# Expert tiles combined at the next head, two extra turns in the routing, first products of the dense layer reordered

## The chip, the cores and the metric

One Trainium2 chip, one of its cores. The metric is the device time of one execution of the whole kernel in microseconds (us), lower is better. The core's engines run each its own queue of instructions in order: TensorE (PE; PEld is its weight loads), VectorE (DVE), ScalarE (ACT), GpSimd (POOL) and SyncE (SP, which here only issues transfers). They wait for each other by semaphores.

## The reference

Three stages follow one another: attention with pooled queries, a mixture of experts in which each token takes part or is skipped, and a gated dense layer.

```python
q_pool = q.reshape(B, H, S // 2, 2, D).mean(axis=3)          # B 4, H 8, S 1152, D 64
scores = (1 / sqrt(D)) * q_pool @ k.T ; attn = softmax(scores)
x = (attn @ v) as [2304, 512]
do_compute = x @ w_skip > 0                                   # of these tokens:
e_idx = argmax(x @ w_gate) over 8 experts, gate_w = its softmax weight
y = gate_w * (relu(x @ w1[e]) @ w2[e])                        # w1[e] 512 x 1024, w2[e] 1024 x 512
x = x + y for these tokens, x for the others
out = ((x @ m1) * (x @ m2)) @ w3 @ w_out                      # 512 -> 1024 -> 1024 -> 512
```

## The kernel before

All products are made from fp32 values split into a high and a low part, and three partial products each (high by high, high by low, low by high).

**Attention.** 16 pairs of heads (`p`) with 9 row tiles each (`l`) give 144 steps `i`; the loop runs some steps longer to drain. In a step PE transposes the exponentials of step i-2 (`emit_t`, L305, evacuated by ACT and DVE at L324), makes one part of attention times values (`emit_pv`, L341), and the scores of step i (`emit_s`, L271), whose maximum DVE takes at L282 and whose exponential ACT makes at L294. PE's order in a step is transposes, values, scores.

**Side work.** Two generators are advanced in small turns between the instructions of the steps. `conv` rewrites the weights of the dense layer, which come in 64-bit pairs, as plain fp32 (POOL squares at L96, DVE at L111 to L119, transfers at L83 and L86). `route_ops(b)` routes the tokens of batch b and writes their rows to `x_d`; it starts in step 44 + 36 b for the batches 0, 1 and 2. It yields "P" ahead of a piece with PE products and "D" ahead of a piece with DVE work alone. `side("D")` is called once in each step, after the second group of transposes: if the routing stands at "D", it advances the routing; if it stands at "P", or no routing is under way, it advances `conv`. `side("P")` is called at the end of the steps with l in 8, 0, 1, 3, 4, 5, if the routing stands at "P", and advances the routing. Its products go to the one of two accumulators (`VB`) that the values don't use at that l.

**One-hot blocks.** For each of five groups of up to 128 tokens `build(j)` makes a block `ob` on POOL (L441 and L444, twice each) that marks slot and order of each token; PE multiplies its two halves (L465), and DVE adds the result into `slots` (L467). Two block buffers exist, so blocks 0 and 1 are built at once, at the end of the last D turn ahead of them, and block j+2 after the product of block j. Then come the softmax weights (a D turn) and five turns in which the tokens' rows are transposed, scaled (L490), joined with the gate weight (L493) and stored. The fourth batch is routed after the loop with a `hook` and five block buffers; its blocks are built on DVE, and its products are at L456.

**Between the stages.** `wprime` multiplies w3 by w_out, and `wprime_fill` splits their weights on POOL, from the last pair of the attention on.

**Experts.** `tiles(j)` is a nest of 25 branches `If(T > j)`, where T is the number of expert tiles of 128 tokens (11 for these inputs). The branch is at L920 on every engine. `tile_body(j)` gathers the rows of tile j+2 by POOL, splits the expert's weights if it is a new one, multiplies (`hmm`, `htr`, `ymm`; PE at L560), and at its end combines: DVE adds gate times product from bank B[5] to the row (L743), and POOL scatters the rows to `x_d` (L744). Behind the last tile, the other branch (`Else`) calls `split_m1`: ACT and DVE split the first weights of the dense layer into `W1`, four pieces of two column blocks each (`split_cols`, L912 on ACT, L913 on DVE).

**Dense layer.** The splits of its second weights into `V2` follow (same two lines). `group(g)` takes 384 tokens: for each of eight column blocks c it makes the product with `W1` in one bank and that with `V2` in the next (L952, 12 matmuls each), multiplies both (ACT L955, DVE L956), and splits the result; then it makes the output products (L560) and scatters the rows. The rows of the next group are gathered at the start of a group (`ld_x`, L615). Group 0 holds tokens without an expert.

Of the kernel before, what the change touches and what calls it, by code (L numbers as in the profile page):

```python
# [44 lines left out]
def body(ctx, tc, q, k, v, w9, w1, w2, m1, m2, w3t, wo, cst, mcst, ids, out, dbg=None):  # L45
# [89 lines left out]
    if True:  # L135
# [217 lines left out]
        def route_ops(b, hook=None, obs=None):  # L353
# [93 lines left out]
            parts = ((0, 0, NSL), (1, NSL, NCNT))  # L447
            for j in range(len(obs)):
                build(j)
            if len(obs) == NTT:  # L450
                yield "P"
                tp = tbank()
                for u, c0, n in parts:
                    for j in range(NTT):
                        t = ob[j]
                        PE.matmul(tp[:, c0:c0 + n], lhsT=t[:, 128 * u:128 * u + 128], rhs=t[:, 256 + c0:256 + c0 + n],  # L456
                                  start=(j == 0), stop=(j == NTT - 1))
                DVE.tensor_tensor(slots, tp[:, 0:NSL + NCNT], slots, op=ALU.add)
            else:
                for j in range(NTT):  # L460
                    yield "P"
                    tp = tbank()
                    t = ob.pop(j)
                    for u, c0, n in parts:
                        PE.matmul(tp[:, c0:c0 + n], lhsT=t[:, 128 * u:128 * u + 128], rhs=t[:, 256 + c0:256 + c0 + n],  # L465
                                  start=True, stop=True)
                    DVE.tensor_tensor(slots, tp[:, 0:NSL + NCNT], slots, op=ALU.add)  # L467
                    if j + len(obs) < NTT:
                        build(j + len(obs))
# [30 lines left out]
        def side(kinds):  # L500
            k = rts.get("k")
            if k and k in kinds:
                rts["k"] = next(rts["g"], None)
            elif k != "D":
                next(conv, None)

        def emit_meta(scratch):
# [184 lines left out]
            DVE.tensor_tensor(XTt[1], b0, f(XTt[0]), op=ALU.subtract)  # L692

        def tile_body(j, x2_first):
            xg = XR[j % 4]
            more = j + 1 < NTILE
            if j + 2 < NTILE:
                gather(j + 2)
            if j + 3 < NTILE:
                ld_idx(j + 3)  # L700
            if j:
                nw = nc.values_load(meta[0:1, j, 0:1], min_val=0, max_val=1)
                with tc.If(nw > 0):
                    split(W2, R2, 8)
                    ld_next(R2, w2, j)

            def hmm(hh, a0, a1):
                for a in range(a0, a1):
                    mm3(B[1 + hh], [XTt[0][:, a], XTt[1][:, a]],
                        [W1[x][:, a, 512 * hh:512 * hh + 512] for x in range(2)], a == 0, a == 3)  # L710
                if a1 == 4:
                    ACT.activation(HS[:, 512 * hh:512 * hh + 512], B[1 + hh], AF.Relu)

            def htr(hh):
                for u in range(4):
                    c = 4 * hh + u
                    PE.transpose(B[3 + hh][:, 128 * u:128 * u + 128], HS[:, 128 * c:128 * c + 128], ident)
                b3 = B[3 + hh].rearrange("p (a c) -> p a c", a=4)
                ACT.copy(HT[0][:, 4 * hh:4 * hh + 4], b3)
                DVE.tensor_tensor(HT[1][:, 4 * hh:4 * hh + 4], b3, f(HT[0][:, 4 * hh:4 * hh + 4]), op=ALU.subtract)  # L720

            def ymm(a0, a1):
                for a in range(a0, a1):
                    mm3(B[5], [HT[0][:, a], HT[1][:, a]], [W2[0][:, a], W2[1][:, a]], a == 0, a == 7)

            hmm(0, 0, 4)
            hmm(1, 0, 2)
            htr(0)
            hmm(1, 2, 4)
            if more:  # L730
                xpose(j + 1)
            if j == 0:
                x2_first()
            ymm(0, 2)
            htr(1)
            if more:
                nw = nc.values_load(meta[0:1, j + 1, 0:1], min_val=0, max_val=1)
                with tc.If(nw > 0):
                    split(W1, R1, 4)
                    ld_next(R1, w1, j + 1, "m1")  # L740
            ymm(2, 4)
            ymm(4, 8)
            DVE.scalar_tensor_tensor(xg[:, 0:D], B[5], xg[:, D:D + 1], xg[:, 0:D], op0=ALU.mult, op1=ALU.add)  # L743
            scs.append(POOL.indirect_dma_start(  # L744
                out=x_d[:, :], out_offset=bass.IndirectOffsetOnAxis(ap=IDX[j % 5][:, :], axis=0),
                in_=xg[:, :], in_offset=None, bounds_check=N - 1, oob_is_err=False).ins)

        with tc.manual_schedule():
# [23 lines left out]
            for i in range(NSTEP + 7):  # L772
# [25 lines left out]
                if tr:  # L798
                    for g in range(3):
                        emit_t(it, g, i, evac)  # L800
                        emit_c(it, g, EV[g], evac)
                        if g == 1 and i > 5:
                            side("D")
                if 1 <= i <= NSTEP:
                    emit_e(i - 1)
                for u in pvs:
# [105 lines left out]
                ACT.copy(W[0][:, :, cols], r[:, :, cols])  # L912
                DVE.tensor_tensor(W[1][:, :, cols], r[:, :, cols], f(W[0][:, :, cols]), op=ALU.subtract)  # L913

            def split_m1():
                for c in range(0, 8, 2):
                    split_cols(W1, R1, c, c + 2)

            def tiles(j):
                with tc.If(T > j) as cmp:  # L920
                    tile_body(j, x2_first)
                    if j + 1 < NTILE:
                        tiles(j + 1)
                    else:
                        split_m1()
                with cmp.Else():
                    if j == 0:
                        x2_first()
                    split_m1()
            tiles(0)  # L930

            V2 = [W2[x].rearrange("p a f -> p (a f)").rearrange("p (a f) -> p a f", a=4) for x in range(2)]
# [11 lines left out]
            def group(g, x2, nx):  # L944
                if nx is not None:
                    ld_x(nx, XR)
                for c in range(8):
                    pa, pb = B[(2 * c) % 4], B[(2 * c) % 4 + 1]
                    for o, W in ((pa, W1), (pb, V2)):
                        seq = [(0, y, a) for a in range(4) for y in range(2)] + [(1, 0, a) for a in range(4)]  # L950
                        for n, (x, y, a) in enumerate(seq):
                            PE.matmul(o[:, 0:GT], lhsT=W[x][:, a, 128 * c:128 * c + 128], rhs=x2[y][:, a],  # L952
                                      start=(n == 0), stop=(n == len(seq) - 1))
                    av, cv = AV[c % 2], CW_[c % 2]
                    ACT.copy(av, pa[:, 0:GT])  # L955
                    DVE.tensor_tensor(cv, pb[:, 0:GT], av, op=ALU.mult)  # L956
                    ACT.copy(CV[0][:, c], cv)  # L957
                    DVE.tensor_tensor(CV[1][:, c], cv, f(CV[0][:, c]), op=ALU.subtract)
                    if g == 0 and nx is not None:
                        ACT.copy(WP[0][:, c], WPr[:, c])  # L960
                        DVE.tensor_tensor(WP[1][:, c], WPr[:, c], f(WP[0][:, c]), op=ALU.subtract)
                    if nx is not None and c in (3, 5, 7):
                        x2t(X2[nx % 2], (c - 3) // 2, XR[(c - 3) // 2])
# [82 lines left out]
```

## Time and profile before

| | |
|---|---|
| median of 3 runs | 1090.47 us (1088.94 to 1090.56) |
| profiled execution | 1092.66 us |
| its span, first to last instruction | 1090.8 us |
| busy: PE, DVE, ACT, POOL | 1038.4, 598.0, 482.4, 387.0 us |
| waits of PE for one-hot blocks (L465) | 5.9 us in 3 |
| wait of PE at the first product of the dense layer (L952) | 4.7 us in 1 |
| granted clock of PE, mean over the span | 0.984 |

Times within the trace count from the span's start. The attention stage runs to about 550 us, the experts' tiles from about 615 to 767 us, the dense layer from there to the end. A busy PE is not PE at its peak, since matmuls are pipelined and their ends are modelled; so the length of a piece of work is best read from the distance between starts of the same instruction in neighbouring steps.

### The profile page before, as it was taken

To read this page: it belongs to the slowest core of one execution; us is meant where nothing else is said; L and a number is where in the kernel's file an instruction comes from. 1 tells how busy PE (TensorE), PEld (TensorE's weight loads), DVE (VectorE), ACT (ScalarE), POOL (GpSimd) and SP (SyncE) were. 2 spreads that over 40 slices of the span, in tenths; PEclk is the share of its full clock that TensorE was granted. 3 is DMA by queue.
4 is the path that set the end of the run, shared out by engine and by line. 5 is a ranking of instruction groups with operands and counts; after the bars stand their busy time and mean duration, and the time that the engine had idled before them with its cause. 6 is when DMAs were issued, how large, how long until landed. Compare 5 with 4: busy or idle time off the path is not lost. (4 is left out here: it accounts for less than half of the span.)

```text
span 1090.8 us, 16927 instructions
## 1 busy us (share of the span) xinstructions
PE 1038.4 (95%) x6101; PEld 839.9 (77%) x6101; DVE 598.0 (55%) x934; ACT 482.4 (44%) x902; POOL 387.0 (35%) x426
## 2 busy tenths in 40 slices
PE   6999999999999999999999999998799999999996
PEld 5677776677766777667667778786799998989895
DVE  5888887688986888755637422437531221212120
ACT  4666666565665666555532322334432221212121
POOL 4754433672536724351620523439201010101101
PEclk9999999999999999989998999999899999999999
DMA  9887778377973678714702761507101010101000
GB/s 256 259 239 192 216 218 232 101 182 212 268 224 98 185 214 256 183 40 101 238 20 74 247 225 40 190 25 243 34 11 50 10 49 20 39 20 39 29 2 30
DMA packets 68237, 144.83 MB, mean 133 GB/s; under 512 B 12960, under 2 KB 22560, under 8 KB 68130
## 3 DMA queue, kind: packets, MB, share of 16 engines
q1 hardware_dynamic: 63330, 129.28, 41.1%
q0 software_dynamic: 4800, 14.24, 4.0%
q8 instruction: 53, 0.87, 0.3%
q14 instruction: 54, 0.44, 0.1%
HBM read 86.21 MB, written 22.87 MB: 100 GB/s over the span
## 5 line engine op out<-in xcount | busy, mean ns | idle before, releaser
L282 DVE TENSOR_REDUCE sm<-s 128x1 f32<-128x1152 f32 x144 | 195.2, 1356 | 108.4 <-PE s L271 88.3
L324 ACT COPY pt<-s 128x384 f32<-128x384 f32 x288 | 138.0, 479 | 184.4 <-PE s L305 184.1
L271 PE MATMUL s<-k,q 128*128 128x384 f32 x864 | 204.3, 364 | 15.5 <-DVE k L197 7.8
L271 PEld LDWEIGHTS s<-k,q 128*128 128x128 f32 x864 | 147.2, 193 | 83.8 <-issue 41.7
L294 ACT ACTIVATE p<-s,sm 128x1152 f32<-128x1152 f32 x144 | 176.3, 1225 | 10.0 <-DVE sm L282 9.7
L341 PE MATMUL vb<-pt,vr 128*64 128x256 f32 (+1 forms) x1152 | 173.9, 422 | 4.5 <-DVE xr L490 2.1
L305 PE MATMUL s<-cs,p 128*128 128x128 f32 x1296 | 172.0, 279 | 2.9 <-ACT p L294 2.9
L305 PEld LDWEIGHTS s<-cs,p 128*128 128x128 f32 x1296 | 151.5, 144 | 12.1 <-ACT p L294 6.2
L956 DVE TENSOR_TENSOR ar<-b,ar 128x384 f32<-128x384 f32 x48 | 26.8, 558 | 191.9 <-PE b L952 191.9
L341 PEld LDWEIGHTS vb<-pt,vr 128*64 128x64 f32 x1152 | 70.7, 137 | 59.4 <-issue 23.7
L971 POOL DMA_INDIRECT out_dram<-ar,slots x18 | 18.1, 1003 | 272.1 <-ACT ar L970 267.4
L324 DVE COPY pt<-s 128x384 f32<-128x384 f32 x144 | 78.9, 548 | 5.1 <-PE s L305 5.0
L225 POOL TENSOR_TENSOR kl<-kr,kh 128x384 fp32r<-128x384 f32 x45 | 47.6, 1058 | 73.0 <-DMA k<-kl 70.2
L957 ACT CAST CVh<-ar 128x384 fp32r<-128x384 f32 x48 | 24.6, 513 | 108.8 <-DVE ar L956 108.8
L96 POOL TENSOR_TENSOR cm<-ch 128x512 f32<-128x512 f32 x40 | 43.0, 1079 | 66.6 <-DVE ca L119 46.1
L560 PE MATMUL b<-W1h,CVh 128*128 128x512 f32 x176 | 60.5, 403 | 1.2 <-ACT CVh L691 0.7
L560 PE MATMUL b<-W2h,CVh 128*128 128x512 f32 x176 | 60.7, 405 | 0.3
L560 PE MATMUL b<-WPh,CVh 128*128 128x512 f32 x144 | 57.3, 398 | 0.0
L560 PE MATMUL b<-WPh,CVl 128*128 128x512 f32 x144 | 56.9, 395 | 0.0
L560 PE MATMUL b<-WPl,CVh 128*128 128x512 f32 x144 | 56.8, 395 | 0.0
L970 ACT COPY ar<-b 128x512 f32<-128x512 f32 x18 | 10.6, 586 | 86.2 <-PE b L560 86.2
L224 POOL TENSOR_SCALAR kh<-kr 128x384 fp32r<-128x384 f32 x45 | 27.2, 604 | 57.2 <-PE s L271 53.6
(210 smaller groups left out, 1816.7 us busy)
## 6 DMA issues: line engine op xcount, KB each, us to landing
R<-in_w_dram SPq DMA_DIRECT2D x16, 1024.0 KB, 7.1
vr<-in_v_dram SPq DMA_DIRECT2D x16, 576.0 KB
kr<-in_k_dram SPq DMA_DIRECT2D x15, 576.0 KB, 6.2
qr<-in_q_dram SPq DMA_DIRECT2D x15, 576.0 KB, 6.6
k<-kh SPq DMA_DIRECT2D x30, 288.0 KB, 5.6
k<-kl SPq DMA_DIRECT2D x30, 288.0 KB, 6.4
q<-qnl SPq DMA_DIRECT2D x60, 144.0 KB, 3.4
ch<-in_w3t_dram SPq DMA_DIRECT2D x16, 512.0 KB, 5.6
```

The costliest lines, as they stand in the source:

```text
L96: POOL.tensor_tensor(m, hf, hf, op=ALU.mult)
L224: POOL.tensor_scalar(KH[i][:, cc], rawk[p][:, cc], 1.0, 0.0, op0=ALU.mult, op1=ALU.add)
L225: POOL.tensor_tensor(KL[:, cc], rawk[p][:, cc], f(KH[i][:, cc]), op=ALU.subtract)
L271: m = PE.matmul(sp[:, c, 0:384], lhsT=lt, rhs=kk[:, 384 * c:384 * c + 384], start=(n == 0), stop=(n == len(seq) - 1))
L282: DVE.tensor_reduce(sm, sp[:, :, 0:384], axis=AX.XY, op=ALU.max, negate=True)
L294: ACT.activation(pt, sp[:, :, 0:384], AF.Exp, bias=sm, scale=1.0, accum_out=SM[b][:, hp, c:c + 1])
L305: m = PE.transpose(tp[:, u * 128:u * 128 + 128], src[:, kt * 128:kt * 128 + 128], ident)
L324: m = (DVE.tensor_copy(o, i_) if eng is DVE else ACT.copy(o, i_)).ins
L341: PE.matmul(acc[64 * h:64 * h + 64, 0:n], lhsT=vr[:, h, kt, :], rhs=pt[:, kt, h, :], start=(kt == 0), stop=(kt == KT - 1))
L560: PE.matmul(o, lhsT=lh[a], rhs=rh[b_], start=(first and n == 0), stop=(last and n == len(order) - 1))
L956: DVE.tensor_tensor(cv, pb[:, 0:GT], av, op=ALU.mult)
L957: ACT.copy(CV[0][:, c], cv)
```

## The change

In the first three batches `route_ops` yields twice more, as "C", between the building of the first two blocks and the first product. `side("DC")` advances the routing at "D" and at "C"; `conv` is advanced in each step's call unless the routing stood at "D" (so in a C turn both are), and not at all by `side("P")`. The end of `tile_body` becomes a function `combine(j)`. It is called at the head of `tile_body(j + 1)`, or, behind the last tile, in `split_m1`, after two pieces of one column block each; the other three pieces follow it. In the group 0 that is followed by another group, PE makes the `W1` products of the blocks 0 and 1 ahead of their `V2` products.

```diff
@@ route_ops, side
             for j in range(len(obs)):
                 build(j)
+            if not hook:
+                yield "C"
+                yield "C"
             if len(obs) == NTT:
@@
             if k and k in kinds:
                 rts["k"] = next(rts["g"], None)
-            elif k != "D":
+            if kinds != "P" and k != "D":
                 next(conv, None)
@@ tile_body
         def tile_body(j, x2_first):
-            xg = XR[j % 4]
+            if j:
+                combine(j - 1)
             more = j + 1 < NTILE
@@
             ymm(2, 4)
             ymm(4, 8)
+
+        def combine(j):
+            xg = XR[j % 4]
             DVE.scalar_tensor_tensor(xg[:, 0:D], B[5], xg[:, D:D + 1], xg[:, 0:D], op0=ALU.mult, op1=ALU.add)
             scs.append(POOL.indirect_dma_start(
@@ the loop over the steps
                         if g == 1 and i > 5:
-                            side("D")
+                            side("DC")
@@ split_m1, tiles
-            def split_m1():
-                for c in range(0, 8, 2):
+            def split_m1(j):
+                split_cols(W1, R1, 0, 1)
+                split_cols(W1, R1, 1, 2)
+                if j >= 0:
+                    combine(j)
+                for c in range(2, 8, 2):
                     split_cols(W1, R1, c, c + 2)
@@
                     else:
-                        split_m1()
+                        split_m1(j)
                 with cmp.Else():
                     if j == 0:
                         x2_first()
-                    split_m1()
+                    split_m1(j - 1)
@@ group
-                for c in range(8):
-                    pa, pb = B[(2 * c) % 4], B[(2 * c) % 4 + 1]
-                    for o, W in ((pa, W1), (pb, V2)):
+                def prods(c, which):
+                    for o, W in ((B[(2 * c) % 4 + u], (W1, V2)[u]) for u in which):
                         seq = [(0, y, a) for a in range(4) for y in range(2)] + [(1, 0, a) for a in range(4)]
...
+                for c in range(8):
+                    pa, pb = B[(2 * c) % 4], B[(2 * c) % 4 + 1]
+                    if g == 0 and nx is not None and c < 2:
+                        if c == 0:
+                            prods(0, (0,))
+                            prods(1, (0,))
+                        prods(c, (1,))
+                    else:
+                        prods(c, (0, 1))
```

## Rows read from the trace of the kernel before

**Rows 1.** The page, busy us (share of the span) and instructions of each engine.
```profile
PE 1038.4 (95%) x6101; PEld 839.9 (77%) x6101; DVE 598.0 (55%) x934; ACT 482.4 (44%) x902; POOL 387.0 (35%) x426
```

**Rows 2.** Waits of PE over the span: us in total, times, longest.
```profile
PE vb L465 <- POOL ob L444: 5.9, 3, 2.0
PE b L952 <- DVE W1l L913: 4.7, 1, 4.7
...
PE vb L456 <- DVE R L444: 1.8, 4, 0.5
```

**Rows 3.** Timeline of PE, first batch: start, us, instruction, idle before and releaser.
```profile
207.96 1.34 PE L271 MATMUL s<-k,q 128*128 128x384 f32 x6
211.29 0.75 PE L465 MATMUL vb<-ob 128*128 128x146 f32 x2 [1.99 <-POOL ob L444]
...
215.60 1.34 PE L271 MATMUL s<-k,q 128*128 128x384 f32 x6
...
218.86 1.34 PE L271 MATMUL s<-k,q 128*128 128x384 f32 x6
...
222.32 0.62 PE L271 MATMUL s<-k,q 128*128 128x384 f32 x2
```

**Rows 4.** The same timeline in the second and in the third batch.
```profile
344.54 1.34 PE L271 MATMUL s<-k,q 128*128 128x384 f32 x6
...
352.15 1.32 PE L271 MATMUL s<-k,q 128*128 128x384 f32 x6
...
481.65 1.34 PE L271 MATMUL s<-k,q 128*128 128x384 f32 x6
...
489.63 2.24 PE L271 MATMUL s<-k,q 128*128 128x384 f32 x6
...
493.80 1.31 PE L271 MATMUL s<-k,q 128*128 128x384 f32 x6
...
497.24 0.62 PE L271 MATMUL s<-k,q 128*128 128x384 f32 x2
```

**Rows 5.** Timeline of POOL, first batch: the building of blocks 0 and 1.
```profile
209.17 1.21 POOL L441 TENSOR_SCALAR ob<-iota,hf 128x128 fp32r<-128x128 f32 x2 [7.51 <-DVE hf L434]
...
210.37 1.29 POOL L444 TENSOR_SCALAR ob<-iota,hf,idf 128x146 fp32r<-128x146 f32 x2
```

**Rows 6.** Stretches: length, busy PE, PEld, DVE, ACT, POOL; granted clock, DMA, GB/s.
```profile
211.30:215.20 3.90, 3.81 (x17) 2.92 (x19) 1.50 (x3) 1.56 (x3) 3.90 (x7) 0.56 0.00 0
...
485.00:491.70 6.70, 6.70 (x25) 5.02 (x26) 1.48 (x3) 2.17 (x4) 5.67 (x9) 0.50 0.38 94
...
580.40:587.30 6.90, 6.44 (x19) 5.18 (x20) 5.15 (x22) 0.00 (x0) 0.00 (x0) 0.51 0.01 2
...
771.80:775.00 3.20, 3.19 (x10) 3.20 (x11) 3.20 (x4) 3.14 (x5) 1.37 (x1) 0.50 0.03 8
```

**Rows 7.** Instructions on tile xr, 230 to 545 us: count, ns least/median/most.
```profile
L493 DVE COPY xr<-ga x15: 151/160/1406, 244.0 to 540.3; 128x4 f32<-128x4 f32 x12, 64x4 f32<-64x4 f32 x3
```

**Rows 8.** Timeline of all engines behind the last tile.
```profile
764.97 3.89 ACT L912 CAST W1h<-R 128x1024 fp32r<-128x1024 f32 x4 [3.32 <-issue]
...
767.15 0.75 DVE L743 SCALAR_TENSOR_TENSOR xr<-b,xr 128x512 f32<-128x512 f32 x1 [4.77 <-PE b L560]
...
770.45 4.63 DVE L913 TENSOR_TENSOR W1l<-R,W1h 128x1024 fp32r<-128x1024 f32 x4 [2.55 <-issue]
...
771.82 0.66 PE L952 MATMUL b<-X2h,W1h 128*128 128x384 f32 x1 [4.71 <-DVE W1l L913]
```

**Rows 9.** Branches of PE's queue at L920: whole span, then 766 to 773 us.
```profile
L920 PEldq COMPARE_BRANCH  x13: 65/70/3672, 614.7 to 770.4; - x13
...
L920 PEldq COMPARE_BRANCH  x2: 179/1926/3672, 766.4 to 770.4; - x2
```

**Rows 10.** Timeline around one tile's end: its sum, and the next product into B[5].
```profile
647.34 0.75 DVE L743 SCALAR_TENSOR_TENSOR xr<-b,xr 128x512 f32<-128x512 f32 x1 [2.77 <-PE b L560]
...
653.54 0.49 PE L560 MATMUL b<-W2h,CVh 128*128 128x512 f32 x1
```

## The prediction, made before the changed kernel was run

> **What bounds the kernel now.** I read the page first: TensorE is busy for 95% of the span [rows 1], so only what leaves TensorE idle, or slows it, is worth anything. Then the waits of TensorE over the whole span: two rows of that list belong to lines that the change touches [rows 2]. One is L465, the products of the one-hot blocks, which waited for the POOL builds three times, 5.9 us in all; the other is L952, the first product of the dense layer, which waited once for 4.7 us. Third, the timeline of TensorE around the three waits, to see what they cost beyond the idle time itself [rows 3, 4]; fourth, the table of stretches for the granted clock behind them [rows 6]; last, the timeline and the branches at the change from the experts to the dense layer [rows 8, 9]. [...] And the 4.7 us at the dense layer are for the most part a jump of TensorE's own queue, which the change doesn't shorten.
>
> **Part 1, the two turns.** In each of the first three batches the last D turn ends with POOL building two one-hot blocks, and the first product follows at the end of the same step (step 55 of 144 in the first batch, by my count of the turns through the loop). POOL starts at 209.17 and ends the four builds of these two blocks at 211.66 [rows 5]; TensorE is idle for 1.99 us until the first block is there [rows 3]. The new "C" turns put two passes of the loop between builds and product, that is two steps of some 3.3 us each, against builds of 2.5 us. The product then finds its block ready, with 4 us to spare. The conversion work that `side` hands out isn't delayed by the turns: the new condition advances it in a C turn too, and the count of D turns is the same.
>
> What this is worth I read from the distance between the first score products (L271) of neighbouring steps. The step without a turn takes 218.86 - 215.60 = 3.26 us, the step with one product 222.32 - 218.86 = 3.46 us [rows 3]. The step with the wait takes 215.60 - 207.96 = 7.64 us, an excess of 4.18. In the second batch it is 352.15 - 344.54 = 7.61, an excess of 4.15; in the third 489.63 - 481.65 = 7.98, an excess of 4.52, and the step behind it takes 493.80 - 489.63 = 4.17 against 3.26, another 0.91 [rows 4]. Sum: 4.18 + 4.15 + 5.43 = 13.76 us. Of this some 6 us are idle time (three times 2.0) [rows 2], and the rest is the clock: granted 0.56 from 211.3 to 215.2, and 0.50 for 6.7 us in the third batch [rows 6], which is why the same wait cost more there.
>
> Where the turns go: the five products move by one or two places, the transposes behind them by one, and the last transpose by three steps, into a place where there was no turn. Each turn costs about what it cost before, so I count that at nothing; what hides it is that blocks three to five are built while the earlier ones are multiplied, at least one step ahead. If POOL were late with one of them, that wait would be a new one of the old price (rival 2). What is queued on POOL behind the later builds is the preparation of the keys of a pair that is needed over half a pair later; DVE waits for nothing new in these steps.
>
> In the third batch there is a price. While POOL splits the weights for the combined product, the small copy L493 takes up to 1.41 us on DVE, where its median is 0.16 [rows 7]. The change keeps full-width copies in these steps and adds one at the end of the last pair. I bound it between 0 and 1.5 us (two copies held as long as the longest would be 2.5, but one of the two stood there before, with half the rows) and take 0.7. [...]
>
> **Part 2, combining at the next head.** `combine` is the same DVE instruction and the same scatter; only the branch L920 moves from behind to ahead of it. Where the tiles go on, the branch is a fall-through: TensorE's median over 13 is 70 ns [rows 9]. The order on DVE and POOL is otherwise unchanged (scatter j, gather j+3 on POOL in both), so I count ten tile heads at nothing. The cover, at one of them: DVE is done with the tile's sum at 648.09, and the first product into that bank comes at 653.54, 5.4 us later [rows 10].
>
> Behind the last tile it is different. DVE could not leave for the other branch before TensorE's last product; it combined at 767.15, sat idle 2.55 us for the jump, and began its first split at 770.45; TensorE's first product came at 771.82, when that split was done [rows 8]. With the change DVE jumps while TensorE still works, splits two columns, and then combines. ACT had its part of the split ready by 766 [rows 8], so the two narrow splits are done at about 767. What is late next is TensorE itself: its own branch takes 3.67 us [rows 9], from 766.37, and a second, short one ends at 770.6. So it can start at about 770.7 rather than at 771.82: 1.1 us. The clock is at 0.50 until 775 [rows 6], ten products in 3.2 us; if it comes back at the same moment as before, the 1.1 us are worth half of that. I take 0.6, with bounds of 0 and 1.1. The added narrow pair of instructions (0.2 us on ACT and DVE) lies beside TensorE.
>
> [...]
>
> **Part 3, the order of the first products.** Two W1 products, then the V2 ones. Before, TensorE had no further wait after its first product there, the only wait of L952 in the list being the 4.7 us [rows 2]. So the order has nothing to hide now; with the earlier start it covers the V2 splits, which DVE ends later than the W1 ones. I count it at nothing, between 0 and 0.5 lost in ACT's and DVE's queue behind it.
>
> **The sum.** 13.76 - 0.7 + 0.6 = 13.7 us. The profiled execution took 1092.66 us, of which the span is 1090.8; the median of the three runs is 1090.47, 2.2 us below it. The gain is a difference of steps and doesn't depend on which of them is taken: 1090.47 - 13.7 = 1076.8, so 1077.
>
> **The rivals.** Rival 1: the idle time goes and the clock stays low. For it: in the last batch, from 580.4 to 587.3, the clock was at 0.51 [rows 6] behind four short waits of at most 0.5 us, those of L456 [rows 2], so it isn't long waits alone. Against it: steps with the same work and no wait run at full clock. Gain 3 x 2.0 + 0.6 = 6.6 us: 1084.
>
> Rival 2: the wait moves. A later block comes late, or another engine's work (DVE's copies) ends last in the step of the product. If it drops the clock in every batch, part 1 gives nothing, and the time is 1090, no change; in one batch, 1081. Against it: before, products of blocks three to five waited for no build, since all three long waits are at the first product [rows 2].
>
> Rival 3: the jump behind the last tile turns out short, as the 70 ns of the other heads. Then TensorE starts at about 767.2 and not at 771.82, which is 4.0 us more than I counted, and the 3.2 us at half clock behind it [rows 6] shrink too, by 1.6: 1071.
>
> Rival 4, slower: the combining at the head holds the tile. Something at the head, the branch or the loads behind it, delays DVE's sum; TensorE waits at the first product into the bank B[5]. It decides from 5.4 us of delay [rows 10]. To be 2.2 us slower in all it would have to take 15.9 us back, 1.6 us at each of ten heads, so 7.0 us of delay at each: 1093. The only thing put ahead is a branch of some 0.07 us.
>
> **How the numbers follow.** Forecast 0.76, alone between 1073.5 and 1080.5 (the third batch's copies, the start of the dense layer, and stretches at half clock that fall differently, since the same wait cost 4.15 us in one batch and 5.43 in another). Rival 1 0.09, rival 2 in one batch 0.05 and in all 0.04, rival 3 0.03, rival 4 0.03. A range from 1073 to 1084 holds the forecast, rival 1's centre and the half of rival 2, and leaves out less than 2 in 10. What a measurement can tell from no change is 0.2%, 2.2 us: faster 0.93, same 0.04, slower 0.03.
>
> **What would show it.** Right: no wait of L465 for POOL over 0.3 us; the three steps at 3.3 to 3.5 us; no row of half clock in the three places; TensorE idle some 3.6 us, not 4.7, ahead of its first L952, with DVE's narrow splits ahead of L743. Wrong: a wait of L465 at a later block, L271 or L341 waiting for DVE in the shifted steps, half clock without a wait, or L952 still waiting for DVE.

## The result, and the profile of the changed kernel

| | before | changed |
|---|---|---|
| median of 4 runs, taken beside each other | 1089.93 us (1088.94 to 1090.56) | 1076.55 us (1074.97 to 1077.09) |
| ratio, 95% interval | | 0.9876 [0.9859, 0.9893] |
| profiled execution, its span | 1092.66, 1090.8 us | 1077.07, 1075.3 us |

The change makes the kernel faster by 13.5 us (1.24% of 1089.93; by the interval 11.7 to 15.4 us), and the time lies 0.45 us below the one predicted. That total hides two errors of opposite sign, which the experiments below take apart. Lines below L450 of the kernel before stand three lines further down in the changed one (L465 is L468), those of `tile_body` four, and those from L743 on seven to twenty (L743 is L750, L744 L751, L913 L920, the branch L920 L931, L952 L962, L955 L975). The kernels of the experiments have their own line numbers.

First the page, then TensorE's waits over the whole span (us in total, times, longest), the rows that answer to [rows 1, 2]:

```profile
PE 1030.2 (96%) x6101; PEld 835.4 (78%) x6101; DVE 592.6 (55%) x935; ACT 482.3 (45%) x903; POOL 390.0 (36%) x426
```

```profile
PE b L962 <- PEq L931: 3.4, 1, 3.4
PE vb L341 <- DVE xr L493: 2.1, 3, 0.7
PE vb L459 <- DVE R L444: 1.9, 4, 0.5
```

The list has no row of L468 for POOL any more: the 5.9 us are gone, and no row of that size stands in their place. L341's 2.1 us for DVE look like a new wait in the shifted steps, but the list of before has the same row:

```profile
PE vb L341 <- DVE xr L490: 2.1, 3, 0.7
```

The wait ahead of the dense layer is 3.4 us and not 4.7, and its releaser is now TensorE's own branch, L931.

The timeline of TensorE in the first batch (start, us, instruction) answers to [rows 3], and the table of stretches to the first of [rows 6] (length; busy PE, PEld, DVE, ACT, POOL; granted clock, DMA share, GB/s):

```profile
207.97 1.34 PE L271 MATMUL s<-k,q 128*128 128x384 f32 x6
211.23 1.34 PE L271 MATMUL s<-k,q 128*128 128x384 f32 x6
214.50 1.33 PE L271 MATMUL s<-k,q 128*128 128x384 f32 x6
215.67 0.28 PE L468 MATMUL vb<-ob 128*128 128x146 f32 x2
217.96 0.62 PE L271 MATMUL s<-k,q 128*128 128x384 f32 x2
```

```profile
211.30:215.20 3.90, 3.90 (x28) 3.17 (x28) 2.96 (x4) 2.90 (x6) 3.90 (x6) 1.00 0.00 0
```

The step that began at 207.96 and took 7.64 us before takes 211.23 - 207.97 = 3.26 us; the two that follow take 3.27 and 3.46. The first product comes at 215.67 with no wait ahead of it. The granted clock is 1.00 where it was 0.56. The answering steps of the second and the third batch take 3.27 us each, and so does the step behind the third (4.17 before).

One of the prediction's signs of being wrong did come, later in the first batch: L271 waits for DVE in a shifted step. The last transposes of the tokens now lie in step 71, and the start of step 72 looks like this, before and in the changed kernel (TensorE, then DVE and POOL):

```profile
274.73 1.32 PE L271 MATMUL s<-k,q 128*128 128x384 f32 x6
...
278.19 1.34 PE L271 MATMUL s<-k,q 128*128 128x384 f32 x6
```

```profile
270.86 0.62 PE L271 MATMUL s<-k,q 128*128 128x384 f32 x2
271.99 0.97 PE L271 MATMUL s<-k,q 128*128 128x384 f32 x4 [0.51 <-DVE pt L324]
...
275.11 1.34 PE L271 MATMUL s<-k,q 128*128 128x384 f32 x6
...
270.26 1.22 DVE L496 COPY xr<-ga 64x4 f32<-64x4 f32 x1
...
270.05 1.41 POOL L230 TENSOR_TENSOR qsum<-qr 128x576 f32<-128x576 f32 x1
```

Step 72 takes 275.11 - 270.86 = 4.25 us in place of 3.46. With the runs of the experiments, the steps 57 to 72 together take 59.27 to 59.35 us in five executions without the turns and 60.60 to 60.65 in nine with them: 1.3 us more, of which 0.2 is the product that moved in from step 55. So the turns have a price of about 1.1 us there.

Behind the last tile (timeline of all engines, answers to [rows 8]; idle time before and releaser in brackets), and the stretches behind it:

```profile
751.41 0.39 PE L563 MATMUL b<-W2h,CVh 128*128 128x512 f32 x1
...
749.78 3.98 ACT L919 CAST W1h<-R 128x512 fp32r<-128x512 f32 x5 [3.42 <-issue]
...
751.28 1.29 DVE L920 TENSOR_TENSOR W1l<-R,W1h 128x512 fp32r<-128x512 f32 x2 [4.21 <-SPq L931]
...
752.50 0.74 DVE L750 SCALAR_TENSOR_TENSOR xr<-b,xr 128x512 f32<-128x512 f32 x1
...
755.22 0.66 PE L962 MATMUL b<-X2h,W1h 128*128 128x384 f32 x1 [3.42 <-PEq L931]
```

```profile
755.20:760.90 5.70, 5.68 (x18) 5.70 (x19) 5.40 (x7) 4.35 (x6) 1.96 (x2) 0.51 0.05 11
760.90:765.00 4.10, 4.10 (x25) 4.10 (x24) 1.30 (x2) 0.01 (x1) 3.49 (x3) 1.00 0.30 70
```

The last tile's last product stood here before:

```profile
766.71 0.40 PE L560 MATMUL b<-W2h,CVh 128*128 128x512 f32 x1
```

DVE's two narrow splits begin at 751.28, ahead of the combining at 752.50, as the diff has it; TensorE starts when its own jump is over. From the last product of the last tile to the first of the dense layer it is 755.22 - 751.41 = 3.81 us (771.82 - 766.71 = 5.11 before), a gain of 1.30. But the clock then stays at half for 5.7 us, where it was 3.2 in [rows 6]. So at the first output product the gain of this pair of executions is only 41.39 - 41.18 = 0.21 us, counted from the last tile's last product.

### The profile page after: what moved, and what is told of

Read it like the earlier page. It is cut to its first block, busy times and chain, and to the rows that moved or that the text cites. A ratio compares the mean times of both kernels' runs of the same rounds, so it can differ in the third digit from the quotient of the medians.

```text
span 1075.3 us, 16933 instructions
## 1 busy us (share of the span) xinstructions
PE 1030.2 (96%) x6101; PEld 835.4 (78%) x6101; DVE 592.6 (55%) x935; ACT 482.3 (45%) x903; POOL 390.0 (36%) x426
## 3 DMA queue, kind: packets, MB, share of 16 engines
q1 hardware_dynamic: 63330, 129.28, 41.4%
## 5 line engine op out<-in xcount | busy, mean ns | idle before, releaser
L271 PE MATMUL s<-k,q 128*128 128x384 f32 x864 | 202.4, 362 | 12.6 <-DVE k L197 7.6
L271 PEld LDWEIGHTS s<-k,q 128*128 128x128 f32 x864 | 146.3, 191 | 79.5 <-issue 40.8
L341 PE MATMUL vb<-pt,vr 128*64 128x256 f32 (+1 forms) x1152 | 171.9, 418 | 4.5 <-DVE xr L493 2.1
L305 PE MATMUL s<-cs,p 128*128 128x128 f32 x1296 | 169.2, 276 | 3.6 <-ACT p L294 3.6
L305 PEld LDWEIGHTS s<-cs,p 128*128 128x128 f32 x1296 | 149.1, 143 | 12.7 <-ACT p L294 6.6
L341 PEld LDWEIGHTS vb<-pt,vr 128*64 128x64 f32 x1152 | 69.8, 136 | 58.2 <-issue 22.1
```

The costliest lines, as they stand in the source:

```text
L271: m = PE.matmul(sp[:, c, 0:384], lhsT=lt, rhs=kk[:, 384 * c:384 * c + 384], start=(n == 0), stop=(n == len(seq) - 1))
L305: m = PE.transpose(tp[:, u * 128:u * 128 + 128], src[:, kt * 128:kt * 128 + 128], ident)
L341: PE.matmul(acc[64 * h:64 * h + 64, 0:n], lhsT=vr[:, h, kt, :], rhs=pt[:, kt, h, :], start=(kt == 0), stop=(kt == KT - 1))
```

## The experiments

Theory: in each batch a 2.0 us wait of TensorE at the first product costs its own length and, behind it, time at half clock; the turns take both away. At the dense layer TensorE's own jump is last. Rivals: the clock drops without these waits too; the gain comes from the combining or the order of the first products; the jump could be hidden. Times below are medians; ratios are against runs of the kernel before on the same chip. In the tables, "step" is the distance between the first score products of neighbouring steps at the old place of the wait, in the three batches.

**Each part alone.** On the kernel before, only the two turns:

```diff
+            if not hook:
+                yield "C"
+                yield "C"
@@
-            elif k != "D":
+            if kinds != "P" and k != "D":
@@
-                            side("D")
+                            side("DC")
```

> Part 1 alone (the two turns; combining and order of products as before). Theory: the turns carry nearly all of the gain, 13 us, so 1077 us, and no wait of PE for a one-hot block over 0.3 us; the first product of the dense layer still waits 4.7 us for DVE. Rival 'the other parts carry it': under 5 us gained, 1085 us or more. Rival 'the clock stays low without the wait': 1084 us, with half clock behind step 55 of the first batch.

Only the combining at the next head, with `split_m1` in the new order, and without the turns and the new order of the first products:

```diff
+            if j:
+                combine(j - 1)
@@
+                split_cols(W1, R1, 0, 1)
+                split_cols(W1, R1, 1, 2)
+                if j >= 0:
+                    combine(j)
```

> Combining at the next head alone (no turns, products in the old order). Theory: PE's own branch (3.4 to 3.7 us) ends last at the dense layer, so PE starts there 1.1 to 1.3 us earlier than before, and the clock takes most of it back: 0.2 to 0.6 us in all, 1089.4 us, not to be told from no change. Rival 'the start is worth its idle time': 1.3 us, 1088.6. Rival 'it costs something at each of ten tile heads': 1091 us or more, with the distances between the tiles longer than the 12.4 us that most of them take.

| | median | ratio [95%] | in us of 1086.8 |
|---|---|---|---|
| turns alone | 1077.45 | 0.9902 [0.9879, 0.9925] | -10.7 (8.2 to 13.2) |
| combining alone | 1084.57 | 0.9976 [0.9963, 0.9990] | -2.6 (1.1 to 4.0) |

The two sum to 13.3 us, what the whole change gives. The turns are most of it, with steps of 3.27 us in all three batches; the 13.1 us predicted for them (13.76 - 0.7) lie at the upper end of the interval. The combining is worth more than the 0.6. With the combining alone TensorE's waits are these:

```profile
PE vb L465 <- POOL ob L444: 5.9, 3, 2.0
PE b L959 <- PEq L928: 3.4, 1, 3.4
```

The wait for the blocks is that of before, the wait at the dense layer that of the changed kernel: the two parts don't touch each other. And this execution shows something that one trace of before couldn't. Its first batch, TensorE's timeline and the stretches:

```profile
205.77 1.34 PE L271 MATMUL s<-k,q 128*128 128x384 f32 x6
...
209.08 0.69 PE L465 MATMUL vb<-ob 128*128 128x146 f32 x2 [1.98 <-POOL ob L444]
211.77 1.32 PE L271 MATMUL s<-k,q 128*128 128x384 f32 x6
```

```profile
209.30:211.30 2.00, 1.92 (x17) 1.50 (x18) 1.09 (x3) 0.91 (x3) 2.00 (x4) 1.00 0.00 0
211.30:215.20 3.90, 3.90 (x30) 2.78 (x27) 2.40 (x4) 2.82 (x6) 3.90 (x7) 1.00 0.00 0
```

The same wait of 1.98 us, and the clock stays at 1.00. The step takes 211.77 - 205.77 = 6.00 us, not 7.64. So the half clock behind this wait isn't bound to follow.

**How long the wait is.** On the kernel before, POOL builds block 0 twice, so the wait grows; or DVE builds block 0, so it shrinks:

```diff
+            if not hook:
+                build(0)
             for j in range(len(obs)):
                 build(j)
```

> The kernel before with block 0 built twice in a row on POOL in the first three batches, so that the first product waits 2.5 us longer (4.5 us). Theory: the wait is paid in full, and the clock behind it once, so each of the three steps grows by 2.5 us, or by up to 1.7 us more where a longer stretch at half clock falls behind it: 1097.5 to 1102.5 us. Rival 'the loss at half clock grows in proportion to the wait': step 55 takes 3.46 + 4.18 x 2.25 = 12.9 us, and the whole 1106 us. Rival 'POOL's builds aren't what PE waits for': 1090 us.

```diff
+                E = DVE if hook or j == 0 else POOL
```

> The kernel before with block 0 alone built on DVE (1.2 us by the durations that these instructions have on DVE in the fourth batch, in place of 2.5 on POOL) in the first three batches, the first product in its old place. Theory: PE's wait falls from 2.0 to some 0.7 to 0.9 us; short waits do not drop the clock by themselves, so each batch gains 1.2 us of idle time and 1.7 to 3.4 us of clock, 9 to 11 us in all: 1079 to 1081 us. Rival 'any wait at this place costs the clock': only the idle time, 3.6 us: 1086 us. DVE's score maxima come 1.2 us later in this step, which could add up to 1 us a batch.

Their waits at the first product, doubled block first, then the block on DVE:

```profile
PE vb L467 <- POOL ob L444: 13.1, 3, 4.4
```

```profile
PE vb L466 <- DVE ob L445: 1.9, 3, 0.6
```

| wait, longest | steps of the three batches | half clock behind it | ratio [95%] |
|---|---|---|---|
| 0.6 us (block on DVE) | 4.78, 4.76, 4.76 us | in none | 0.9921 [0.9897, 0.9946] |
| 2.0 us (before, the profile of the first section) | 7.63, 7.61, 7.98 | in all three | 1 |
| 2.0 us (combining alone) | 6.01, 6.88, 7.10 | in two | 0.9976 [0.9963, 0.9990] |
| 2.0 us (before once more, below) | 6.74, 5.99, 7.60 | in two | 1.0018 [1.0000, 1.0035] |
| 4.4 us (block 0 twice) | 10.40, 10.38, 10.38 | in all three | 1.0087 [1.0065, 1.0110] |

The row of the longest wait, from the stretches behind it:

```profile
213.70:216.90 3.20, 3.20 (x15) 1.79 (x13) 1.24 (x2) 2.17 (x4) 3.20 (x6) 0.50 0.00 0
```

The step without half clock grows by the wait itself: 4.77 us with 0.64 us of wait, 6.00 with 1.98, so 1.23 us for 1.34. The step with 4.4 us of wait would by that take 8.4 us and takes 10.4: 2.0 us are the clock, and the step behind it takes 3.8 to 4.2 us in place of 3.26, another 0.6 to 0.9. The time of that kernel, 1097.08 us, lies just below the range expected. A wait of 0.6 us never cost clock, one of 4.4 us always, and one of 2.0 us sometimes. These are three places in each kernel.

**The kernel before once more**, word for word, beside itself, since the combining alone had shown that the old attention varies:

> The kernel before once more, for a third trace of the same waits. Theory: the three waits are again 2.0 us each, the three steps take 6.0 us where no half clock falls behind the wait and up to 7.7 us where it does, so the attention stage varies by some 5 us between executions of one kernel. Rival 'the half clock always follows the wait': 7.6 us or more in each of the three steps.

It measured 1089.86 (8 runs) against 1087.88 (15 runs): 1.0018 [1.0000, 1.0035]. So two series of one kernel differ by 2 us on one chip, and an edit worth less than that isn't settled by one such comparison; the combining's 2.6 us are little more. Its three waits are again 5.9 us in 3, its steps 6.74, 5.99 and 7.60 us: half clock in two of the three. The stretch from step 30 to the last step of the attention takes 430.55 us in the profile of before, 424.81 in this one and 426.09 with the combining alone. With the turns it takes 415.69 to 416.20 us in nine executions, 415.92 in the changed kernel. So the turns save 8.9 to 14.6 us, and most of the spread is the old attention's.

**The changed kernel again, with the order of the first products undone, and with one turn.**

> The changed kernel once more, on the chip and beside the runs of the other three of this call. Theory: what the kernel before loses to the clock behind the three waits differs from run to run (one trace of it lost 1.7, 1.7 and 3.4 us of it, another, with the same waits, 0, 0.9 and 1.5), so the gain has a fixed part of 3 x 2.5 = 7.6 us and a part of 0 to 6; with 0.2 to 1 us at the dense layer 8 to 14 us in all. Rival 'the gain is 13.7 us wherever it is measured': a ratio of 0.987 to 0.988 again.

```diff
-                    if g == 0 and nx is not None and c < 2:
+                    if False:
```

> The changed kernel with the first products of the dense layer in the old order (part 3 undone). Theory: DVE has split the first columns of V2 by the time that PE has done 12 products, so the order hides nothing: the same as the changed kernel within 0.5 us, and no second wait at L962. Rival 'the order fills a wait for V2': a wait of 0.5 to 2 us at the first V2 product, and as much longer.

```diff
             if not hook:
                 yield "C"
-                yield "C"
```

> The changed kernel with one C turn in place of two. Theory: the step behind the builds has l = 2, in which no product is placed, so with one turn the first product falls in the same step 57 as with two, block 0 is ready, and steps 55, 56 and 57 are as long as with two turns: the same as the changed kernel. Rival 'the second turn is needed': a wait of L467 for POOL of 0.3 us or more.

| | median | ratio [95%] |
|---|---|---|
| changed kernel again | 1076.3 | 0.9891 [0.9864, 0.9918] |
| order undone (same chip) | 1073.82 | 0.9874 [0.9844, 0.9903] |
| one turn (another chip) | 1075.07 | 0.9874 [0.9847, 0.9901] |

The order of the first products gives nothing that can be seen. With the old order the first output product comes 40.58 us behind the last tile's last product (40.79 with the combining alone), with the new one 40.18 to 41.18. (That the median is lower by 2.5 us is within both intervals; in its profile the tiles 6 to 9, counted from 0, take 49.72 us and not 51.83, for a reason that the last experiment touches.) One turn does what two do: steps of 3.27 us in all three batches, and no wait for POOL. The product can't run in the step right behind the turn, since `side("P")` isn't called at l = 2, and step 56 has l = 2. So the second turn stands where nothing could have run anyway.

**The last batch.** From 580.4 to 587.3 the clock was at 0.51 behind four short waits [rows 6]; rival 1 of the prediction leaned on it. In the changed kernel it is the same (first row below). With more pieces of the combined product (w3 by w_out) put ahead of the one-hot products of that batch, on the changed kernel:

```diff
-            pieces = {0: 1, 2: 1, 4: 3, 5: 3}
+            pieces = {0: 1, 2: 1, 4: 3, 5: 6}
```

> The changed kernel with six in place of three pieces of the combined product (w3 by w_out) ahead of the one-hot products of the fourth batch; the pieces are taken from a later place. Theory: there, too, small waits on the blocks (four of 0.3 to 0.5 us, 1.9 us in all) are followed by half clock (5.7 us of it in the trace of the changed kernel). With DVE's blocks ready, waits and half clock go: 2 to 5 us less than the changed kernel. Rival 'PE waits later instead': the pieces that are missing behind uncover the loading and splitting of the first expert's weights, a wait of 2 to 4 us ahead of the first expert product, and no gain.

It measured 1075.66, 0.9886 [0.9859, 0.9913], the same as the changed kernel. The stretch of these products in the changed kernel, and in this one:

```profile
566.50:573.40 6.90, 6.70 (x20) 5.50 (x21) 5.12 (x20) 0.00 (x0) 0.00 (x0) 0.52 0.01 2
```

```profile
564.00:571.00 7.00, 7.00 (x39) 5.97 (x39) 5.84 (x23) 1.86 (x4) 0.00 (x0) 1.00 0.01 2
```

```profile
PE b L692 <- DMA xr<-x_d,ix: 6.0, 1, 6.0
```

The half clock is gone there, and the last of the combined product's pieces is done 4.3 us earlier than in the second profile of the changed kernel (6.6 than in the first). All of it is handed back: the first tile's transposes wait 6.0 us for the gathered rows. The chain products, slots, list of tiles, gather sets the start of the experts: POOL begins the first gather at 595.23 here and at 594.90 in the first profile of the changed kernel. TensorE only had less to do meanwhile.

**The jump behind the last tile.** POOL makes its share of the split of the expert's second weights ahead of the scatter and the gather, on the changed kernel:

```diff
             if j:
-                combine(j - 1)
+                combine(j - 1, 1)
...
                     split(W2, R2, 8)
                     ld_next(R2, w2, j)
+                combine(j - 1, 2)
+            if j + 2 < NTILE:
+                gather(j + 2)
```

(`combine(j, 1)` is DVE's sum, `combine(j, 2)` POOL's scatter.)

> The changed kernel with POOL's part of the W2 split ahead of the scatter and the gather at the tile head (DVE's sum stays first). Theory: PE's waits for the W2 split (3.2 us in four) go, and behind the last tile PE's queue reaches its branch some 3 us earlier, so that most of the jump of 3.4 to 3.7 us lies beside products that are still queued: PE idle under 1.5 us at the first product of the dense layer, and 3 to 8 us less than the changed kernel with the half clock behind it. Rival 'the later gather holds the next tile': PE waits at L692 for gathered rows, and no gain. Rival 'the jump is no shorter for starting earlier': 2 us less, and PE still idle for 3.4 us.

It measured 1077.31, 0.9904 [0.9879, 0.9930]: no gain. TensorE's waits, and the instructions of DVE's split over the whole span (count; ns least, median, most) here and in the changed kernel:

```profile
PE b L563 <- DVE CVh L725: 7.6, 3, 3.5
...
PE b L966 <- DVE W1l L924: 0.8, 1, 0.8
```

```profile
L684 DVE TENSOR_TENSOR W2l<-R,W2h x20: 677/1103/1785, 601.6 to 746.5; 128x512 fp32r<-128x512 f32 x20
```

```profile
L684 DVE TENSOR_TENSOR W2l<-R,W2h x20: 676/680/1791, 602.4 to 742.7; 128x512 fp32r<-128x512 f32 x20
```

The jump is now hidden: 0.8 us of idle time at the first dense product in place of 3.4. But DVE's pieces take 1.10 us in the median where they took 0.68, with POOL splitting at the same time, and TensorE waits 7.6 us for the low parts of the hidden values, which are queued on DVE behind these pieces. The changed kernel has both lengths in one execution: five of these pieces take 3.09 us from 721.81 on, while POOL only scatters, and 5.67 from 737.72 on, while POOL splits the first weights (L686 and L687, until 742.24). Small copies of DVE, too, end together with an instruction of POOL where they are long (last section). Why is not shown.

The other cure takes one piece from POOL and gives it to ACT and DVE, six to two in place of five to three:

```diff
-                if k < 5:
+                if k < (6 if n == 8 else 5):
```

> The changed kernel with six of the eight pieces of the W2 split on ACT and DVE and two on POOL, in place of five and three. Theory: POOL ends 1.9 us earlier behind the head of the last tile, PE's waits for W2 (3.2 us in four) fall below 1 us, and its branch starts some 2 us earlier, so PE is idle for 1.5 to 2.5 us in place of 3.4 at the dense layer; DVE's part of the transposed h comes up to 1.2 us later at two or three tiles: 1 to 3 us less than the changed kernel. Rival 'DVE takes the place': PE's waits for DVE's half of h (L724) grow by 1 us or more a tile, and no gain.

> The kernel with the weight split of 6 pieces on ACT and DVE and 2 on POOL once more, word for word. If the start of the dense layer is what it saves, the distance from the last tile's last product to the first output product is again near 38.4 us against 40.2 to 41.2 in the changed kernel, no wait for POOL's pieces is over 0.5 us, and the ratio to the kernel before is again about 0.985 (0.982 to 0.988). If the 4 us below the changed kernel were the luck of fewer half-clock stretches, the distance is again above 40 us and the ratio near 0.989.

| | median | ratio [95%] |
|---|---|---|
| split six to two | 1070.66 | 0.9850 [0.9827, 0.9873] |
| the same again | 1071.84 | 0.9846 [0.9829, 0.9864] |

Both series lie below all series of the changed kernel (1076.55, 1076.3; one turn, beside the first of the two: 1075.07) and that with the order undone (1073.82), though the intervals of the ratios just touch. This version beats both kernels, by about 16.5 us against before and, by an estimate from these medians and ratios, some 3 to 5 against the changed one. Where that comes from: in the changed kernel TensorE waits four times for POOL's part of the second weights (W2), in two rows of its list that neither series' profile has:

```profile
PE b L563 <- POOLq L742: 1.6, 2, 0.9
PE b L563 <- POOL W2l L687: 1.6, 2, 1.2
```

Two scatters make POOL late, the fifth and the ninth of the eleven. They take 3.66 us each in the changed kernel, and 4.27 in the second series' profile. The ninth in both, and DVE's pieces of the same split beside it:

```profile
722.17 3.66 POOL L751 DMA_INDIRECT x_d<-xr,ix  x1 [3.90 <-DVE xr L750]
...
721.81 3.09 DVE L684 TENSOR_TENSOR W2l<-R,W2h 128x512 fp32r<-128x512 f32 x5
```

```profile
721.77 4.27 POOL L751 DMA_INDIRECT x_d<-xr,ix  x1 [3.90 <-DVE xr L750]
...
721.41 3.68 DVE L684 TENSOR_TENSOR W2l<-R,W2h 128x512 fp32r<-128x512 f32 x6
```

The scatter ends 0.94 us behind the last of DVE's pieces, with five of them as with six. So the piece moved from POOL to DVE goes with a scatter that is 0.6 us longer, and POOL, which has one piece less, is done earlier all the same.

The second weights of the last two tiles are split behind the ninth scatter. A tile without such a wait takes 12.4 us from end to end. With three pieces on POOL the last but one takes 14.23 and the last 17.14 us in the changed kernel. With two pieces, in the second series' profile, they take 12.77 and 15.84, though the scatter was slower still: 2.8 us. Tile 5, behind the fifth scatter, takes 12.41 in place of 13.48. In some executions these scatters took 1.25 us (order undone and block on DVE both of them, the first series here the ninth). The whole way from tile 5 to the last tile is 82.5 us in the changed kernel, 78.8 with three pieces and quick scatters, 78.3 in the second series and 77.6 in the first. So with slow scatters the split takes out 4.2 us. Quick scatters alone take out 3.7, and the first series, with one of them quick, lies 1.2 below that. Part of what one profile gains there is therefore the scatter's.

The idle time of TensorE at the dense layer, which I expected to shrink to 1.5 to 2.5 us, did not: it is 3.2 and 3.0 us. In the first series TensorE's second branch ended at 748.06, 1.9 us ahead of its first product, and what it waits for is DVE's first split:

```profile
PE b L962 <- DVE W1l L920: 3.2, 1, 3.2
```

What I expected of the second series, the first output product again at 38.4 us behind the last tile's last product, was a miss too: it came at 40.95, since there the clock was at half for 5.8 us behind the idle time and in the first series it wasn't:

```profile
750.00:755.00 5.00, 5.00 (x29) 5.00 (x30) 5.00 (x6) 3.84 (x6) 1.28 (x1) 1.00 0.05 9
```

```profile
751.60:757.40 5.80, 5.75 (x18) 5.79 (x19) 5.80 (x7) 4.08 (x6) 1.29 (x1) 0.50 0.06 14
```

The ratio held without it. So, as far as two profiles show it, the gain is for the larger part the waits for POOL, and the clock at the dense layer is luck on top.

## Why the prediction was right, point by point

**Part 1.** The mechanism was right, and rival 1 (clock low without the wait) and rival 2 (the wait moves) fell: with the turns no execution had half clock or a wait for POOL at the three places. Of rival 2 there is only the 0.51 us for DVE in step 72, and no half clock behind it. The size was off, at two steps of the working.

The first is the sentence "The gain is a difference of steps and doesn't depend on which of them is taken". The 13.76 us were taken from one execution, of 1092.66 us, where all those of that kernel lie between 1083.3 and 1093.4, and with half clock behind all three waits. Read in the same way, the two other executions of the old attention give 10.7 and 10.8 us. Without half clock the step takes 6.00 us against 3.46 for a step with a product, an excess of 2.5. So 3 x 2.5 = 7.6 us come with the waits themselves, and the rest, 6.1, 3.1 and 3.2 us in the three executions, is the clock's.

The second is "Each turn costs about what it cost before, so I count that at nothing". The steps 57 to 72 take about 1.1 us more in all nine executions with the turns than the moved work explains, as shown above. By the runs part 1 is worth 10.7 us (8.2 to 13.2).

**The price in the third batch** (0.7 us for L493) was looked for in the wrong place. In the third batch two copies of over 1.2 us stand in the changed kernel (1.21 and 1.28) and two stood there before (1.41, the longest of [rows 7], and 1.25), and the fourteen steps from 129 to the last take 52.9 to 53.4 us in nine executions with the turns and 52.7 to 54.3 in five without: nothing to be seen. In the first batch no copy took over 0.16 us before; the last one takes 1.22 now, and DVE comes late for the step behind it. It ends 0.02 us behind the end of POOL's L230, which had begun 0.2 us ahead of it. All the long copies of all runs end like that, right behind an instruction of POOL (last section).

**The row of POOL's builds.** I read [rows 5] as the four instructions of both blocks. They are block 0 alone (two of L441, two of L444); block 1 is built behind it, up to 214.1. It changed no number, since only block 0 is waited for, but "builds of 2.5 us" is one block's, and the slack of block 1 was smaller than I thought. One turn turned out to be enough even so.

**Part 2.** The step "TensorE is last, by its own branch" was right: L962 waits for L931, and it starts 1.30 us earlier, against 1.1 worked out. Over the executions the first product comes 5.11 to 5.26 us behind the last tile's last one with the old order of combining (five) and 3.78 to 4.21 with the new (six). Five of these six lists name L931; that of the changed kernel again names DVE's split (3.8 us), but its two narrow pieces had ended at 752.1 there, and TensorE's second branch at 754.87, 0.24 us ahead of the product. Rival 3 (a short jump) fell. What I took off that, half of it for the clock, was mis-sized in the other direction, and so were the bounds of 0 and 1.1: the time at half clock isn't fixed in place. Over the executions with the old and the new order of combining, the first output product comes 41.4 to 42.8 us behind the last tile's last product (five, mean 42.1) and 40.2 to 41.2 (six, mean 40.6), so 1.5 us. The single pair of the first section, with 0.21, would have misled. Where the rest of the 2.6 us (1.1 to 4.0) of the combining alone lies isn't settled; 1.5 is inside its interval.

**Part 3 and the tile heads** were counted at nothing. The order undone shows no loss, and the tiles 1 to 4 take 49.72 us before and 49.70 in the changed kernel; rival 4 fell. (One tile head of one execution is an exception: with the combining alone, tile 1 took 13.04 us in place of 12.4.)

**The sum** came out because part 1 was some 2.4 us too large (13.1 against 10.7) and part 2 some 1 to 2 us too small. That the time lies within half a microsecond of the forecast is luck; that the waits and their half clock went is not. The range was wide enough for either error.

## What to carry to other kernels

A wait that a step of slack removes was worth here about its own length (2.5 us of step for 2.0 us of wait), and the time at half clock behind it only as an average (6.1, 3.1 and 3.2 us over the three batches, in three executions): read that from several executions, and don't take the slowest one's steps for the gain. Look also at what the shifted work lands beside: here the price was paid where a small copy came to stand next to POOL's work (1.22 us in place of 0.16), in a batch that the prediction hadn't looked at. When a wait at a change of stages is freed, look at what is last next (here TensorE's own jump of 3.4 us, then POOL's share of a split) before moving more work; a share moved from POOL to ACT and DVE gained (0.9850 and 0.9846 against 0.9876 and 0.9891) where an order that made POOL and DVE work side by side did not (0.9904). And a gap that was filled ahead of a chain of transfers gave nothing, since the chain didn't start earlier: the 4.3 to 6.6 us came back as a wait of 6.0.

## What the runs showed of the hardware

- The granted clock behind one and the same wait of 2.0 us differs between executions and between batches: 1.00 in two of the nine places with that wait, at half for a time in seven. Behind 0.6 us it never fell (three places), behind 4.4 us always (three). What the clock cost in the three batches together was 3.1 to 6.1 us in the three executions.
- Idle time of 3.0 us at the dense layer was followed by 5.8 us at half clock (0.50) in one execution of the six-to-two split, and 3.2 us by none in the other (1.00 from 750 to 755).
- Two of the eleven indirect scatters, whose median is 1.04 us, begin 0.36 us behind DVE's split of the second weights. In 21 of 26 such cases they ended 0.94 us behind the last of DVE's pieces (3.66 us with five pieces, 4.27 with six); in the other five they took 1.25 beside the same pieces. Where POOL split first and scattered later they took 1.33 and 1.32. Why the five were quick stays open.
- DVE's split of 128 x 512 values takes 0.68 us in the median of 20 in the changed kernel (the second weights, L684), and 1.10 in the run in which POOL splits its share of them beside it.
- The small copy of 128 x 4 values on DVE takes 0.16 us in the median. In the fourteen executions 37 of these copies took over 0.4 us (up to 2.34), and each of them ended 0.02 to 0.03 us behind the end of an instruction of POOL; six of the 37 stand in the two profiles of the first section, three before (1.41, 1.25 and 0.45 us) and three in the changed kernel (1.22, 1.21 and 1.28).
